# Block-sparse attention and a rational FFN on one core: other PSUM banks for the first scores, paired reads of block numbers, unit factors in one operation

## The chip, the cores and the metric

One core of a Trainium2 chip runs the whole program. The metric is the time of one execution in device microseconds. Three runs of the kernel before gave 828.69, 829.16 and 830.58 us, so the median is 829.16 us.

## The reference

```python
B, H, S, D = 4, 8, 768, 64            # query, key, value; blocks of 32 rows, 24 blocks
scores = q @ k.T / sqrt(D)
mask = near (|i-j| <= 1) | first and last block row and column | 3 sampled blocks per query block
attn = softmax(where(mask, scores, -1e9)) @ v
x = attn.transpose(0, 2, 1, 3).reshape(3072, 512)
h = x @ w_in                          # 512 -> 2048
P = a0 + a1*h + a2*h*h + a3*h*h*h
Q = 1 + |b0|*|h| + |b1|*h*h
out = (P / (Q + 1e-6)) @ w_out        # 2048 -> 512
```

The weights arrive as 64-bit floats and are decoded on the chip.

## The kernel before, in words

The work has three kinds. **Attention** takes two query blocks at a time, a "part" (x = 0, 1, 2, ...; 14 parts per batch, of which three share the two edge blocks that see all keys). For each part PE writes scores into two PSUM banks (`scores`, L817), DVE adds the bias and takes maxima (`maxima`, L829), ACT takes exponentials (L848), PE turns the probabilities (`turn`, L894) and multiplies them with the values (`values`, L940), DVE normalises (L966), PE turns the result (L978), and ACT and DVE write it as two f16 halves, `xh` (L150) and `xl` (L989). In batch 0 the keys of the sampled blocks are copied by POOL from SBUF (`copies`, L761); in later batches SP gathers them. The values are always gathered by SP (L919). Block numbers for both are read from the tile `ix` into registers by a TENSOR_LOAD (`sampled_rows`, L711), one per part and engine, six numbers each.

The **FFN** works on chunks of 256 tokens (c = 0 to 11) in 16 units each (`unit`): the first product in three f16 passes into a bank `ph` (`into`, L1036 to L1038, two halves e = 0, 1), then about ten DVE and ACT operations (L1043 to L1081) that make `gh` (L1071) and `gl` (L1081), then the second product into `acc` (`out_high`, L1093 and L1095; `out_low`, L1099). Four factors per unit (unit scale times 1, |b0|, a1, a3) stand in the tile `fc`, which `factors` fills with four DVE operations per group of units (L1010). There are seven such groups: four of two units each in batch 0, one of eight elements per row for each later batch.

The **weights** are decoded between 17 and 215 us: rows of w_in and w_out pass through DVE (L441, L444, L447) and through conversions that may go to ACT, DVE or POOL (`times`, L150, L152, L154; POOL also L461 and L519).

PSUM has eight banks: two for `acc`, two for `ph`, three named `m` that scores and every transpose share, and one for `av`. Keys of batch 0 are transposed in `ph` banks at the very start; after that the `ph` banks stand unused until the first `into`.

The order on each engine is set ahead of time by a list scheduler in the kernel (`issue`): each `Op` has an engine or several, a price in ns, predecessors, a priority, and slots in rings (`r_sp` for the three `m` banks, `r_ph` for the two `ph` banks). Engines then run their lists strictly in that order. Until the second product begins, the scheduler also puts idle products of an identity on PE (`fill`, L162).

Of the kernel before, what the change touches and what calls it, by code (L numbers as in the profile page):

```python
# [11 lines left out]
F32 = mybir.dt.float32  # L12
# [5 lines left out]
ALU = mybir.AluOpType  # L18
# [6 lines left out]
def kernel(  # L25
# [27 lines left out]
    nc = tc.nc  # L53
    B, H, S, D = q.shape
    DM, DFF = out.shape[1], w_out.shape[0]
    P = 128
    BLK = 32
    NB = S // BLK
    NR = sampled_blocks.shape[1]
# [16 lines left out]
    const = ctx.enter_context(tc.tile_pool(name="const", bufs=1))  # L76
# [8 lines left out]
    ps_h = ctx.enter_context(tc.tile_pool(name="ps_h", bufs=2, space=PSUM))  # L85
# [11 lines left out]
    VE, SC, PO, TE, SY = "DVE", "Activation", "Pool", "PE", "SP"  # L97
# [176 lines left out]
    r_ph, r_sp, r_acc = Ring([None] * 2), Ring(range(3)), Ring([None])  # L274
    r_pr, r_st, r_pT, r_av = Ring([None] * 3), Ring([None] * 4), Ring([None] * PT), Ring(range(2))
# [9 lines left out]
    ix = const.tile([1, NB, NR], I32, name="ix")  # L285


    par = const.tile([P, 8], F32, name="par")
    absb = const.tile([P, 2], F32, name="absb")
    bias = const.tile([P, NB, NS], F32, name="bias")  # L290

    def load_small():
# [4 lines left out]
    def setup():  # L297
        nc.vector.tensor_scalar(out=ix, in0=samp[0:1].rearrange("p i (n w) -> p i n w", w=2)[:, :, :, 0],
                                scalar1=0, scalar2=NB - 1, op0=ALU.max, op1=ALU.min)
        nc.scalar.activation(out=absb, in_=par[:, 4:6], func=AF.Abs)  # L300

        sf = work[:, 2 * NR * NB:3 * NR * NB].rearrange("p (n i) -> p n i", n=NR)
        nc.vector.tensor_copy(out=sf, in_=samp.rearrange("p i (n w) -> p n i w", w=2)[:, :, :, 0])
        ii = work[:, 5 * NR * NB:5 * NR * NB + NB]
        nc.gpsimd.iota(ii, pattern=[[1, NB]], base=0, channel_multiplier=0, allow_small_or_imprecise_dtypes=True)
        dup = work[:, 3 * NR * NB:4 * NR * NB].rearrange("p (n i) -> p n i", n=NR)
        tmp = work[:, 4 * NR * NB:5 * NR * NB].rearrange("p (n i) -> p n i", n=NR)
        for r in range(NR):
            nc.vector.tensor_tensor(out=dup[:, r], in0=sf[:, r], in1=ii, op=ALU.subtract)
        nc.vector.tensor_tensor(out=dup, in0=dup, in1=dup, op=ALU.mult)  # L310
        nc.vector.tensor_scalar(out=dup, in0=dup, scalar1=1.0, scalar2=None, op0=ALU.is_le)
        for edge in (0.0, NB - 1.0):
            nc.vector.tensor_scalar(out=tmp, in0=sf, scalar1=edge, scalar2=None, op0=ALU.is_equal)
            nc.vector.tensor_tensor(out=dup, in0=dup, in1=tmp, op=ALU.max)
        for r in range(1, NR):
            for e in range(r):
                nc.vector.tensor_tensor(out=tmp[:, r], in0=sf[:, r], in1=sf[:, e], op=ALU.is_equal)
                nc.vector.tensor_tensor(out=dup[:, r], in0=dup[:, r], in1=tmp[:, r], op=ALU.max)
        nc.vector.memset(bias, 0.0)
        nc.vector.memset(bias[:, 1, NR:NR + 1], NEG)  # L320
        nc.vector.memset(bias[:, NB - 2, 1:2], NEG)
        for r in range(NR):
            for e in range(2):
                nc.vector.tensor_scalar(out=bias[:, 1 - e:NB:2, r + 5 * e], in0=dup[:, r, 1 - e:NB:2], scalar1=NEG, scalar2=None, op0=ALU.mult)

    s_work = Slot(r_rr)
    o_small = Op(SY, [(475, 1), (475, 1), (475, 1)], load_small, prio=-99, takes=[s_work])
    o_setup = Op(VE, 5300, setup, [o_small], prio=-70, uses=[s_work])


# [43 lines left out]
    banks = [ps_m.tile([P, 512], F32, name=f"m{i}") for i in range(3)]  # L374
# [13 lines left out]
    wscale = const.tile([P, NU], F32, name="wscale")  # L388
# [148 lines left out]
    def block(j):  # L537
        return j + 1 if j < J else 0 if j == J else NB - 1 if j == J + 1 else j - 1
# [12 lines left out]
    kts, xscales, ks_of, v_inv, v_scale, k_done, s_scr, k_evac = {}, {}, {}, {}, {}, {}, {}, {}  # L551
# [10 lines left out]
    def new_pr():  # L562
        return p3.tile([P, 2, 2, NS * BLK], F32, name="pr")
# [135 lines left out]
    parts = []  # L699
    for b in range(B):  # L700
        for j in range(0, NB, 2):
            n = NB // NS if j == J else 1
            parts += [(b, j, s, n) for s in range(n)]
    NX = len(parts)
    rows_of, has = {}, {}

    def sampled_rows(x, eng=mybir.EngineType.SP):

        if (x, eng) not in rows_of:
            i = block(parts[x][1])  # L710
            rows_of[x, eng] = nc.values_load_multi_w_load_instructions(  # L711
                ix[0:1, i:i + 2].rearrange("p i n -> p (i n)"), engines=[eng], min_val=0, max_val=NB - 1,
                skip_runtime_bounds_check_because="clamped when ix was written")[1]
        return rows_of[x, eng]

    def fresh(kind, x, slot):
# [15 lines left out]
    def attention(b, j, prio):  # L732

        i = block(j)
        xs = [x for x, p in enumerate(parts) if p[:2] == (b, j)]
        n = len(xs)
# [3 lines left out]
        prio = [prio + 0.05 * m for m in range(n)]  # L740
        omax, oexp = [], [[], []]
        prs = {}
        for m, x in enumerate(xs):
            def one(m, x):
                p = prio[m]
                s_sp, s_pr = [Slot(r_sp), Slot(r_sp)], Slot(r_pr)
                near = x < KX
                deps = [Q["oq"]]
                kslots = []
                h = {}  # L750
# [42 lines left out]
                    kslots = [s_kg]  # L793

                def scores():
                    h["sp"] = [banks[z.buf].rearrange("p (e s r) -> p e s r", e=2, r=BLK) for z in s_sp]
                    for e in range(2):
                        if near and n > 1:
                            pieces = [(slice(0, NS), kall[:, m * NS:(m + 1) * NS])]
                        elif n > 1:  # L800
                            pieces = [(slice(0, NS), kgs[s_kg.buf][:, 0:NS])]
                        elif near:
                            own = [kxs[:, s_kx.buf, e], kall[:, 0:NB:NB - 1], kall[:, i - 1 + e:i + 2 + e]]
                            pieces, at = [], 0
                            for kx in own if e == 0 else own[1:] + own[:1]:
                                pieces.append((slice(at, at + kx.shape[1]), kx))
                                at += kx.shape[1]
                        elif e == 0:
                            pieces = [(slice(0, NS), kgs[s_kg.buf][:, 0:NS])]
                        else:  # L810
                            pieces = [(slice(0, 2), kgs[s_kg.buf][:, NR:NR + 2]), (slice(2, NS), kgs[s_kg.buf][:, NR + 3:])]
                        q0 = (j + e) % TB * BLK
                        for sl, kx in pieces:
                            for h4 in range(HG):
                                for g in range(2):
                                    rows = slice(g * D, (g + 1) * D)
                                    nc.tensor.matmul(h["sp"][g][h4 * BLK:(h4 + 1) * BLK, e, sl], Q["q"][rows, h4, q0:q0 + BLK], kx[rows, :, h4],  # L817
                                                     start=True, stop=True)
                    if m == 0:
                        d["st"] = p4.tile([P, 40], F32, name="st")  # L820
                    prs[x] = new_pr()

                def maxima(e):
                    def run():
                        st = d["st"]
                        add = bias[:, i + e] if n == 1 else bias[:, 0, 0:1].broadcast_to([P, NS])
                        for g in range(2):
# [5 lines left out]
                    return run  # L833

                o = chain["sc"] = sc_of[x] = Op(TE, 1050 if near else 880, scores, deps, p, behind=chain.get("sc"), takes=s_sp + [s_pr] + ([s_st] if m == 0 else []),
                                     uses=kslots + [Q["slot"]] + ([] if m == 0 else [s_st]))
                o.work = 0.4 if near else 1.0
# [14 lines left out]
                return s_pr, exps  # L852

            d[m] = one(m, x)

        def larger(m):
# [6 lines left out]
        for m, x in enumerate(xs):  # L863
            s_pr, exps = d[m]
# [90 lines left out]
        p = prio[-1] + 3 * 0.1  # L955
# [46 lines left out]
    fcs, o_fc, accs, s_acc, kept = {}, {}, {}, {}, {}  # L1002

    def factors(b, u, n, after, prio):

        def run():
            if b not in fcs:
                fcs[b] = p2.tile([P, 4, NU], F32, name="fc")
            for j, coef in enumerate((1.0, absb[:, 0:1], par[:, 1:2], par[:, 3:4])):
                nc.vector.tensor_scalar(out=fcs[b][:, j, u:u + n], in0=wscale[:, u:u + n], scalar1=v_inv[b], scalar2=coef, op0=ALU.mult, op1=ALU.mult)  # L1010
        for x in range(u, u + n):
            o_fc[b, x] = None
        o = Op(VE, 700, run, after + [o_fc.get((b, 0))], prio)
        for x in range(u, u + n):
            o_fc[b, x] = o

# [169 lines left out]
    for b in range(B):  # L1186
        if b:
            prep(b, when(b))
        for t in range(NT):
            x0 = min(x for x, p in enumerate(parts) if p[0] == b and p[1] // TB == t)  # L1190
            before = prep_q(b, t, -78.95 if b == t == 0 else part_prio(x0) - (3.23 if x0 >= need[0] else 12.17), before)
            for j in range(t * TB, (t + 1) * TB, 2):
                x = next(x for x, p in enumerate(parts) if p[:2] == (b, j))
                attention(b, j, part_prio(x))

    for c, u in order:
        b = c // NCH
# [48 lines left out]
```

## Time and profile before

| | us |
|---|---|
| median of three runs | 829.16 |
| the profiled execution | 828.6 |
| its span, first to last instruction | 826.8 |
| PE busy | 770.6 (93%) |
| DVE busy | 674.9 (82%) |
| ACT busy | 569.7 (69%) |
| POOL busy | 107.5 (13%) |

The profile shows one execution. An engine's busy share is an average over stages with different limits: a share for a stretch is read from the windows below. Where a wait has several causes, the view of waits names the one that came last.

### The profile page before, as it was taken

Reading aid. Unit: us, or ns where it says so; the run is one execution under the profiler, and the core shown is the slowest. Engines: PE = TensorE matmul, PEld = TensorE weight load, DVE = VectorE, ACT = ScalarE, POOL = GpSimd, SP = SyncE. Lnnn points to the kernel's source line nnn. Section 1 sums busy time; section 2 is a strip of 40 time slices with the busy share of each in tenths; the row PEclk is TensorE's granted clock in tenths of the full one; section 3 lists DMA queues with packets and bytes.
Section 4 is the critical chain, followed back from the end, with each engine's and each line's share of the span. In section 5 each row is a group of like instructions: output and inputs, shape, how many; then the busy total and the mean of one; then the engine's idle time right before and its main releaser. Section 6 shows DMA issues by size and latency. Waiting matters only on the chain.

```text
span 826.8 us, 27468 instructions
## 1 busy us (share of the span) xinstructions
PE 770.6 (93%) x10859; PEld 557.3 (67%) x10943; DVE 674.9 (82%) x1580; ACT 569.7 (69%) x1264; POOL 107.5 (13%) x149
## 2 busy tenths in 40 slices
PE   8798918898999999999999999999999999999997
PEld 4556605676677768677777767677777767767774
DVE  2788999899988885788878884887888886887886
ACT  2676777677866769677576759676676758766563
POOL 3547485613100000000000000000000000000000
PEclk9999969899999999999999999999999999999999
DMA  7988874537566957545636757635555436220000
GB/s 210 242 220 238 233 231 138 163 87 189 142 154 165 214 162 194 162 123 162 160 108 164 191 145 196 173 96 157 144 151 149 117 111 182 76 65 2 1 26 26
DMA packets 224416, 121.29 MB, mean 147 GB/s; under 512 B 62624, under 2 KB 214048, under 8 KB 224288
## 3 DMA queue, kind: packets, MB, share of 16 engines
q1 hardware_dynamic: 223136, 115.34, 51.6%
q0 software_dynamic: 1152, 4.19, 1.6%
q8 instruction: 86, 1.41, 0.8%
q14 instruction: 42, 0.34, 0.1%
HBM read 108.47 MB, written 11.01 MB: 145 GB/s over the span
## 4 chain that ended last, share of the span: by engine, by line
PE 81%; DVE 7%; DMA 4%; issue 3%; ACT 2%; POOL 2%; SPq 1%; ACTq 0%; POOLq 0%; DVEq 0%
PE acc L1093 11%; PE ph L1036 9%; PE acc L1095 9%; PE acc L1099 9%; PE ph L1037 9%; PE ph L1038 9%; PE m L817 7%; PE av L940 6%; PE m L894 6%; PE acc L162 3%; DMA vg<-in_v_dram 2%; PE m L556 2%; DMA wl<-in_moe_w_out_dram 1%; PE m L978 1%; POOL wo_h L154 1%
## 5 line engine op out<-in xcount | busy, mean ns | idle before, releaser
L1037 PE MATMUL ph<-xl,wi 128*128 128x256 f16 x768 | 210.5, 274 | 3.1 <-DVE xl L989 3.1
L1036 PE MATMUL ph<-xh,wi 128*128 128x256 f16 x768 | 210.9, 275 | 1.4 <-DVE tt L1053 1.4
L1038 PE MATMUL ph<-xh,wi 128*128 128x256 f16 x768 | 210.7, 274 | 0.0
L1043 ACT ACTIVATE sq<-ph,fc 128x512 f32<-128x512 f32 x96 | 65.9, 687 | 112.6 <-PE ph L1038 112.4
L1093 PE MATMUL acc<-wo_h,gh 128*128 128x512 f32 x384 | 114.5, 420 | 18.7 <-DVE gh L1071 18.0
L848 ACT ACTIVATE pr<-pr,st 128x256 f32<-128x256 f32 x224 | 110.7, 501 | 14.3 <-DVE st L860 14.3
L1060 DVE SCALAR_TENSOR_TENSOR ab<-sq,absb,ab 128x512 f32<-128x512 f32 x96 | 73.2, 763 | 37.1 <-ACT ab L1057 36.9
L829 DVE CUSTOM_DVE_ANT_1 pr<-m,bias 128x256 f32<-128x256 f32 x224 | 83.2, 418 | 22.3 <-PE m L817 22.1
L1099 PE MATMUL acc<-wo_b,gl 128*128 128x512 bf16 x368 | 95.4, 379 | 3.4 <-issue 2.1
L1095 PE MATMUL acc<-wo_l,gh 128*128 128x512 bf16 x316 | 86.5, 384 | 4.6
L1036 PEld LDWEIGHTS <-wi 128*128 128x128 f16 x768 | 75.9, 99 | 21.4 <-issue 5.1
L1071 DVE SCALAR_TENSOR_TENSOR gh<-tt,par,rr 128x512 fp32r<-128x512 f32 x96 | 72.3, 753 | 19.8 <-ACT rr L1067 11.2
L1093 PEld LDWEIGHTS acc<-wo_h,gh 128*128 128x128 f32 x384 | 66.0, 191 | 32.7 <-issue 19.6
L150 ACT ACTIVATE pT<-m 128x512 f32<-128x512 f32 x112 | 64.1, 596 | 34.0 <-PE m L894 32.7
L1037 PEld LDWEIGHTS <-wi 128*128 128x128 f16 x768 | 75.6, 98 | 12.7 <-issue 0.2
L1038 PEld LDWEIGHTS <-wi 128*128 128x128 f16 x768 | 75.5, 98 | 12.6 <-issue 3.4
L1047 ACT ACTIVATE tt<-ph,par,fc 128x512 f32<-128x512 f32 x96 | 74.8, 779 | 0.3 <-DVE gl L1081 0.2
L1050 DVE TENSOR_TENSOR tt<-tt,sq 128x512 f32<-128x512 f32 x96 | 66.9, 697 | 9.4 <-ACT tt L1047 9.4
L1057 ACT ACTIVATE ab<-ph,fc 128x512 f32<-128x512 f32 x96 | 65.6, 683 | 11.2 <-DVE tt L1077 10.5
L1077 DVE SCALAR_TENSOR_TENSOR tt<-tt,par,ab 128x512 f32<-128x512 f32 x96 | 72.2, 752 | 0.5
L894 PE MATMUL m<-ident,pr 128*128 128x128 f32 x448 | 69.6, 288 | 2.9 <-ACT kt L150 2.3
L1053 DVE SCALAR_TENSOR_TENSOR tt<-ph,fc,tt 128x512 f32<-128x512 f32 x96 | 71.4, 744 | 0.8
(130 smaller groups left out, 1221.7 us busy)
## 6 DMA issues: line engine op xcount, KB each, us to landing
vg<-in_v_dram SPq DMA_DIRECT2D x312, 64.0 KB, 2.9
vg<-in_v_dram SPq DMA_DIRECT2D x88, 192.0 KB, 3.6
kall<-ks SPq DMA_DIRECT2D x138, 64.0 KB, 1.9
wl<-in_moe_w_out_dram SPq DMA_DIRECT2D x16, 512.0 KB, 4.8
vg<-in_v_dram SPq DMA_DIRECT2D x12, 512.0 KB, 5.1
kall<-ks SPq DMA_DIRECT2D x23, 256.0 KB, 3.7
ldq<-in_q_dram SPq DMA_DIRECT2D x20, 256.0 KB, 3.4
out_dram<-ld SPq DMA_DIRECT2D x20, 256.0 KB, 2.4
```

The source lines that it names most:

```text
L829: nc.vector.tensor_tensor_reduce(out=prs[x][:, e, g].rearrange("p (s r) -> p s r", r=BLK), in0=h["sp"][g][:, e], in1=add.rearrange("p (s o ...
L848: nc.scalar.activation(out=prs[x][:, e, g], in_=prs[x][:, e, g], func=AF.Exp, scale=SCALE, bias=st[:, 12 + y:13 + y], accum_out=st[:, 16 + ...
L894: nc.tensor.transpose(pp[:, jj * P:(jj + 1) * P], pr[:, e, g, kt:NS * BLK:2], ident)
L1036: nc.tensor.matmul(o, wh, xh[:, :, cc], start=(cc == 0), stop=False)
L1037: nc.tensor.matmul(o, wh, xl[:, :, cc], start=False, stop=False)
L1038: nc.tensor.matmul(o, wl, xh[:, :, cc], start=False, stop=(cc == NCC - 1))
L1047: nc.scalar.activation(out=d["tt"], in_=d["ph"], func=AF.Identity, scale=d["cst"][:, 3:4], bias=par[:, 2:3])
L1060: nc.vector.scalar_tensor_tensor(out=d["ab"], in0=d["sq"], scalar=absb[:, 1:2], in1=d["ab"], op0=ALU.mult, op1=ALU.add)
L1071: nc.vector.scalar_tensor_tensor(out=d["gh"], in0=d["tt"], scalar=par[:, 0:1], in1=d["rr"], op0=ALU.add, op1=ALU.mult)
L1093: nc.tensor.matmul(acc, g, wo_h[:, f], start=(new and e == 0), stop=False)
L1095: nc.tensor.matmul(acc, g, wo_l[:, f], start=False, stop=False)
L1099: nc.tensor.matmul(acc, g, wo_b[:, f], start=False, stop=(last and e == 1))
```

## The change

Three edits:

1. The scores of parts 0 to 4 go to the two `ph` banks instead of to two of the three `m` banks, so that in those parts transposes have the three `m` banks to themselves.
2. One TENSOR_LOAD reads twelve block numbers for two successive parts where the parts' blocks follow each other; the second part then issues none. SP has 24 such loads where it had 44, POOL 6 where it had 11.
3. `factors` is one operation over a `[128, 4, n]` tile in place of four, from a new tile `coefs` that `setup` fills with four small DVE operations; its price in the scheduler is 180 ns where it was 700.

```diff
@@ -287,6 +287,7 @@
 
     par = const.tile([P, 8], F32, name="par")
     absb = const.tile([P, 2], F32, name="absb")
+    coefs = const.tile([P, 4], F32, name="coefs")
     bias = const.tile([P, NB, NS], F32, name="bias")
 
     def load_small():
@@ -298,6 +299,10 @@
         nc.vector.tensor_scalar(out=ix, in0=samp[0:1].rearrange("p i (n w) -> p i n w", w=2)[:, :, :, 0],
                                 scalar1=0, scalar2=NB - 1, op0=ALU.max, op1=ALU.min)
         nc.scalar.activation(out=absb, in_=par[:, 4:6], func=AF.Abs)
+        nc.vector.memset(coefs[:, 0:1], 1.0)
+        nc.vector.tensor_copy(out=coefs[:, 1:2], in_=absb[:, 0:1])
+        nc.vector.tensor_copy(out=coefs[:, 2:3], in_=par[:, 1:2])
+        nc.vector.tensor_copy(out=coefs[:, 3:4], in_=par[:, 3:4])
 
         sf = work[:, 2 * NR * NB:3 * NR * NB].rearrange("p (n i) -> p n i", n=NR)
         nc.vector.tensor_copy(out=sf, in_=samp.rearrange("p i (n w) -> p n i w", w=2)[:, :, :, 0])
@@ -708,9 +713,13 @@
 
         if (x, eng) not in rows_of:
             i = block(parts[x][1])
-            rows_of[x, eng] = nc.values_load_multi_w_load_instructions(
-                ix[0:1, i:i + 2].rearrange("p i n -> p (i n)"), engines=[eng], min_val=0, max_val=NB - 1,
+            two = x + 1 < NX and parts[x + 1][0] == parts[x][0] and parts[x + 1][3] == 1 and block(parts[x + 1][1]) == i + 2
+            got = nc.values_load_multi_w_load_instructions(
+                ix[0:1, i:i + (4 if two else 2)].rearrange("p i n -> p (i n)"), engines=[eng], min_val=0, max_val=NB - 1,
                 skip_runtime_bounds_check_because="clamped when ix was written")[1]
+            rows_of[x, eng] = got[:2 * NR]
+            if two:
+                rows_of[x + 1, eng] = got[2 * NR:]
         return rows_of[x, eng]
 
     def fresh(kind, x, slot):
@@ -743,7 +752,8 @@
         for m, x in enumerate(xs):
             def one(m, x):
                 p = prio[m]
-                s_sp, s_pr = [Slot(r_sp), Slot(r_sp)], Slot(r_pr)
+                early_x = x < 5
+                s_sp, s_pr = [Slot(r_ph if early_x else r_sp) for _ in range(2)], Slot(r_pr)
                 near = x < KX
                 deps = [Q["oq"]]
                 kslots = []
@@ -793,7 +803,7 @@
                     kslots = [s_kg]
 
                 def scores():
-                    h["sp"] = [banks[z.buf].rearrange("p (e s r) -> p e s r", e=2, r=BLK) for z in s_sp]
+                    h["sp"] = [(ps_h.tile([P, 512], F32, name="ph") if early_x else banks[z.buf]).rearrange("p (e s r) -> p e s r", e=2, r=BLK) for z in s_sp]
                     for e in range(2):
                         if near and n > 1:
                             pieces = [(slice(0, NS), kall[:, m * NS:(m + 1) * NS])]
@@ -1006,11 +1016,11 @@
         def run():
             if b not in fcs:
                 fcs[b] = p2.tile([P, 4, NU], F32, name="fc")
-            for j, coef in enumerate((1.0, absb[:, 0:1], par[:, 1:2], par[:, 3:4])):
-                nc.vector.tensor_scalar(out=fcs[b][:, j, u:u + n], in0=wscale[:, u:u + n], scalar1=v_inv[b], scalar2=coef, op0=ALU.mult, op1=ALU.mult)
+            nc.vector.scalar_tensor_tensor(out=fcs[b][:, :, u:u + n], in0=coefs.rearrange("p (j o) -> p j o", o=1).broadcast_to([P, 4, n]), scalar=v_inv[b],
+                                           in1=wscale[:, u:u + n].rearrange("p (o u) -> p o u", o=1).broadcast_to([P, 4, n]), op0=ALU.mult, op1=ALU.mult)
         for x in range(u, u + n):
             o_fc[b, x] = None
-        o = Op(VE, 700, run, after + [o_fc.get((b, 0))], prio)
+        o = Op(VE, 180, run, after + [o_fc.get((b, 0))], prio)
         for x in range(u, u + n):
             o_fc[b, x] = o
 
```

Because prices and rings change, the scheduler sets another order on every engine from about the first score on. Counted over the whole program: PE has 134 idle products where it had 135 (127 where it had 128 ahead of the first `into`). Seven weight conversions more are on POOL (10 `wi<-wo`, 14 `dw<-wi` and 10 `wo_h<-dw` where there were 7, 12 and 8); DVE has five fewer (two `dw<-wi`, one `dw<-wl`, one `wi<-wo_l`, one cast to `wo_h`), ACT two fewer. After the 1146th of DVE's 1553 instructions the orders are alike.

The first place is DVE's, where the first factors of batch 0 stand just behind the scale of the values (`sc`) and ahead of the first `xl`. Before:

```order
L356 TENSOR_SCALAR sc_1035<-sc_1035 128x1
L660 COPY xscale<-sc_1035 128x1
L1010 TENSOR_SCALAR fc<-wscale,sc_1035 128x2
L1010 TENSOR_SCALAR fc<-wscale,sc_1035,absb 128x2
L1010 TENSOR_SCALAR fc<-wscale,sc_1035,par 128x2 x2
L498 TENSOR_REDUCE sums<-sums 128x1
L966 TENSOR_TENSOR xn<-av,st 128x256
L989 SCALAR_TENSOR_TENSOR xl_117<-m_102,xscale,xh_116 128x512
```

And with the change:

```order
L361 TENSOR_SCALAR sc_1057<-sc_1057 128x1
L665 COPY xscale<-sc_1057 128x1
L1019 SCALAR_TENSOR_TENSOR fc<-coefs,sc_1057,wscale 128x4x2
L503 TENSOR_REDUCE sums<-sums 128x1
L976 TENSOR_TENSOR xn<-av,st 128x256
L999 SCALAR_TENSOR_TENSOR xl_118<-m_102,xscale,xh_117 128x512
```

Nothing moved here; four operations became one, with two tensors from SBUF as inputs where each of the four had one.

The second place is also DVE's: the fourth `xl`, which completes the input of chunk 1 and so lets PE begin that chunk's first product. Before, it is instruction 310 of DVE's list, 52 behind the fourth `gh`:

```order
L355 TENSOR_SCALAR scw<-scw 128x1
L356 TENSOR_SCALAR scw<-scw 128x1
L872 TENSOR_SCALAR st<-st 128x4
L502 COPY wscale<-scw 128x1 x2
L875 RECIPROCAL st<-st 128x4
L1010 TENSOR_SCALAR fc<-wscale,sc_1035 128x2
L1010 TENSOR_SCALAR fc<-wscale,sc_1035,absb 128x2
L1010 TENSOR_SCALAR fc<-wscale,sc_1035,par 128x2 x2
L989 SCALAR_TENSOR_TENSOR xl_119<-m_103,xscale,xh_118 128x512
```

With the change it is instruction 279, 21 behind the fourth `gh`:

```order
L976 TENSOR_TENSOR xn<-av,st 128x256
L452 SCALAR_TENSOR_TENSOR wi<-wo_b,wi 128x512
L449 SCALAR_TENSOR_TENSOR wi<-wo_l,wi 128x512
L446 TENSOR_SCALAR wi<-wi 128x512
L452 SCALAR_TENSOR_TENSOR wi<-wo_l,wi 128x512
L449 SCALAR_TENSOR_TENSOR wi<-wo_b,wi 128x512
L999 SCALAR_TENSOR_TENSOR xl_120<-m_103,xscale,xh_119 128x512
```

The maxima of the next part, two groups of factors, the sums of a softmax and seven decoding steps stood ahead of it and now stand behind it.

The third place is PE's, the second product of unit 2 of chunk 0 (the third pass through L1093). Before, it follows straight on the last product of unit 1:

```order
L1099 LDWEIGHTS gl
L1099 MATMUL acc<-wo_b,gl 128x512
L1093 MATMUL acc<-wo_h,gh 128x512 x4
L1095 LDWEIGHTS gh
L1095 MATMUL acc<-wo_l,gh 128x512
```

With the change:

```order
L1109 LDWEIGHTS gl
L1109 MATMUL acc<-wo_b,gl 128x512
L904 MATMUL m_102<-ident,pr 128x128 x8
L950 MATMUL av<-vg_113,pT 32x64 x32
L904 MATMUL m_102<-ident,pr 128x128 x4
L561 MATMUL m_102<-ident,ld 128x128 x4
L950 MATMUL av<-vg_111,pT 32x64 x32
L1103 MATMUL acc<-wo_h,gh 128x512 x4
```

Turns and value products of the edge part, which came after that product, now come ahead of it.

## Rows read from the trace of the kernel before

**Rows 1.** Busy us of PE, PEld, DVE, ACT, POOL by stretch; clock, DMA share, GB/s.

```profile
60.00:80.00 20.00, 16.95 (x348) 12.62 (x347) 17.22 (x45) 12.86 (x33) 17.24 (x27) 0.97 0.77 225
80.00:160.00 80.00, 53.46 (x920) 38.87 (x923) 72.95 (x162) 57.96 (x137) 50.26 (x46) 0.84 0.67 195
160.00:235.00 75.00, 70.71 (x1022) 51.49 (x1019) 74.44 (x164) 55.91 (x120) 15.91 (x15) 1.00 0.56 145
235.00:310.00 75.00, 74.34 (x1076) 54.49 (x1083) 64.02 (x162) 50.81 (x113) 0.00 (x0) 1.00 0.70 174
310.00:750.00 440.00, 432.96 (x6075) 319.53 (x6130) 347.14 (x822) 316.68 (x711) 0.00 (x0) 1.00 0.52 142
```

**Rows 2.** Waits of PE from 60 to 235 us: total, times, longest.

```profile
PE acc L1093 <- DVE gh L1071: 18.0, 2, 17.6
PE ph L1037 <- DVE xl L989: 3.1, 1, 3.1
...
PE m L894 <- ACT kt L150: 2.3, 1, 2.3
```

**Rows 3.** The chain that ended last, 101 to 122 us: start, us, what.

```profile
101.42 7.89 POOL wo_h L154
...
113.87 0.65 POOL dw L154
...
114.55 0.87 DVE dw L441
...
121.28 0.67 DVE gh L1071
```

**Rows 4.** Busy time of line L1010 (factors) alone, by stretch.

```profile
50.00:62.00 12.00, 4.70 (x8) 1.00 0.78 198
130.00:150.00 20.00, 3.61 (x8) 0.84 0.52 144
220.00:225.00 5.00, 0.80 (x4) 1.00 0.45 137
398.00:401.00 3.00, 0.80 (x4) 1.00 0.66 181
584.00:588.00 4.00, 0.81 (x4) 1.00 0.59 168
```

**Rows 5.** Line L1010 over the span: shortest, median and longest in ns.

```profile
L1010 DVE TENSOR_SCALAR fc<-wscale,sc x7: 216/226/958, 53.0 to 585.4; 128x2 f32<-128x2 f32 x4, 128x8 f32<-128x8 f32 x3
L1010 DVE TENSOR_SCALAR fc<-wscale,sc,absb x7: 274/280/1201, 53.6 to 585.6; 128x2 f32<-128x2 f32 x4, 128x8 f32<-128x8 f32 x3
```

**Rows 6.** DVE in order of time, one decoding step twice.

```profile
107.20 0.68 DVE L447 SCALAR_TENSOR_TENSOR wi<-wo_b,wi 128x512 int32<-128x512 int32 x1
...
109.76 1.75 DVE L444 SCALAR_TENSOR_TENSOR wi<-wo_b,wi 128x512 int32<-128x512 int32 x1
```

**Rows 7.** DVE's conversions by line: busy us, mean ns, idle before.

```profile
L154 DVE TENSOR_SCALAR dw<-wi,scw 128x512 f32<-128x512 f32 x4 | 4.9, 1239 | 3.4 <-POOL wi L519 2.0 <-POOL wo_l L461 1.4
L154 DVE TENSOR_SCALAR dw<-wl 128x512 f32<-128x512 f32 x2 | 1.9, 956 | 0.0
L154 DVE TENSOR_SCALAR wi<-wo_l 128x512 f32<-128x512 f32 x2 | 1.2, 584 | 0.0
L152 DVE CAST wo_h<-dw 128x512 fp32r<-128x512 f32 x2 | 0.8, 404 | 0.0
```

**Rows 8.** POOL's conversions to wo_h over the span: shortest, median and longest in ns.

```profile
L154 POOL TENSOR_SCALAR wo_h<-dw x8: 618/1048/7886, 82.2 to 208.4; 128x512 fp32r<-128x512 f32 x8
```

**Rows 9.** PE's idle products ahead of the first product, in order of time.

```profile
59.52 2.76 PE L162 MATMUL acc<-ident 128*128 128x512 f16 x12
...
65.86 0.27 PE L1036 MATMUL ph<-xh,wi 128*128 128x256 f16 x1
```

**Rows 10.** The loads of block numbers: shortest, median, longest.

```profile
L711 SPq TENSOR_LOAD <-ix x44: 1262/1273/1710, 11.1 to 689.2; - x44
L711 POOLq TENSOR_LOAD <-ix x11: 1384/1391/1634, 14.2 to 155.1; - x11
```

**Rows 11.** PE's only wait for gathered values, of the whole span.

```profile
PE av L940 <- DMA vg<-in_v_dram: 0.2, 1, 0.2
```

**Rows 12.** DVE behind the setup, in order of time.

```profile
11.65 0.69 DVE L152 COPY kall<-ph 128x512 f32<-128x512 f32 x1 [2.50 <-PE ph L556]
...
20.59 0.42 DVE L829 CUSTOM_DVE_ANT_1 pr<-m,bias 128x256 f32<-128x256 f32 x1 [5.77 <-PE m L817]
```

## The prediction, as it was put on record before any run of the change

> **What bounds the kernel now.** I read the busy time by stretch first. From 235 us on, PE is busy for all but a few us: 74.3 of 75, then 433.0 of 440 [rows 1]. That part is a fixed amount of PE work, and only what happens before it can move its start. Before it, PE is idle for 33.9 us between 60 and 235 us (3.0, 26.5 and 4.3 in the three stretches), while DVE is busy for 147.4 of the 155 us from 80 to 235 us [rows 1]. So the early part is DVE's, and the reader should see there an engine that does three jobs at once: decoding weights, maxima of attention, and the FFN's element-wise work.
>
> Then the waits: over half of PE's idle time is one wait of 17.6 us for `gh`, the first factor of the second product; behind it come 3.1 us for `xl` and 2.3 us for a turned key [rows 2]. Last, the chain through the long wait: a POOL conversion that took 7.89 us where its like take 1.05 [rows 3, 8], then a conversion on POOL, a decoding step on DVE that needs it, and the `gh` that stands behind that in DVE's list [rows 3]. So PE's wait is DVE's lateness, and some of DVE's lateness is POOL's.
>
> **The change, part by part.**
>
> Factors. Twenty-eight DVE operations go and seven come. The five groups ahead of 235 us are busy for 4.70 (two groups), 3.61 (two groups) and 0.80 us, 9.1 in all; the other two, at 0.80 and 0.81 us, lie where DVE has over 90 of 440 us free and PE sets the pace, so they cost nothing now and give nothing back [rows 1, 4]. Undisturbed, a group takes 0.80 us, as the third row has it [rows 4]. The first four groups took 8.31 us, 2.1 each, while POOL was at work beside them; the shortest single operation was 0.22 us, the longest 1.20 [rows 5].
>
> The trace has no operation like the new one, so I bound it: from below by the shortest factor operation, 0.22 us [rows 5]; from above by a DVE step that normally takes 0.68 us and took 1.75 beside POOL [rows 6]. Five of them cost 1.1 to 8.75 us. I take 0.6 us each, 3.0 in all, near the lower end: it has 8 to 32 elements per row, and in the first four groups more than half of the time is disturbance, which one operation meets once where four met it up to four times. Gain 9.1 - 3.0 = **6.1 us**, with 8.0 and 0.4 as ends.
>
> The row of 1.20 us shows that a factor operation with one tensor input already waits for POOL [rows 5]. [...]
>
> The four small operations in the setup cost DVE some 0.5 us, and they wait for |b|, under 1 us more. DVE waits 2.50 us for PE before the second key tile, and 5.77 us before the first maxima [rows 12]; the cover is larger than the cost, so I take 0. Without that cover it would be 1.5 us.
>
> Weight conversions that change engine. DVE loses five: two at 1.24 us, and 0.96, 0.58 and 0.40 [rows 7], 4.4 us. POOL gains seven. Each may hold up one DVE step, by nothing or by as much as the 1.07 us by which one step was stretched from 0.68 to 1.75 [rows 6], 0 to 7.5 us. I take the middle, 3.7, because rows of both kinds stand side by side. Net gain **0.7 us**, with 4.4 and -3.1 as ends.
>
> Banks. Ahead of the first product at 65.86 us the scheduler fills PE's free time with idle products, such as 12 of them in 2.76 us just before the sixth part's scores [rows 9]. If transposes had been in the scores' way, fewer of them would be left with the change; but the new order has 127 of them ahead of that product where there were 128. So the PE time up to the first product hardly changes: 0, with a gain of 1 as the end. The risk is that the first product needs a `ph` bank that the scores of part 4 still hold; those scores were done 6 us before it [rows 9], so I count nothing.
>
> Block numbers. Forty-four loads of 1.27 us on SP become 24, and 11 of 1.39 us on POOL become 6 [rows 10]. No row shows a load of twelve numbers. Between the same time and twice it, SP's sum goes from 56 us to between 31 and 61, and POOL's from 15 to between 8 and 17. Who would feel it? PE waited for gathered values once, 0.2 us [rows 11], and POOL has 30 of 80 us free between 80 and 160 us [rows 1]. I take 0, with a loss of 1.4 as the end (the first pair's copies land later by one load).
>
> The order. The turns and value products placed ahead of the third second product run inside PE's 17.6 us wait instead of behind it, and the fourth `xl` comes 31 instructions earlier relative to the fourth `gh`. DVE's total of work does not change by that, so in a stretch that DVE bounds I count 0. The end on the good side is PE's waits there, 3.1 + 2.3 = 5.4 us [rows 2].
>
> **The sum.** 6.1 + 0.7 = 6.8 us. The profiled execution took 828.6 us (span 826.8), 0.6 us below the median of 829.16. 828.6 - 6.8 = 821.8; on the median's scale **822.4 us**. The ends of the terms that don't exclude each other give 816 to 828 for this case.
>
> **The rivals.**
>
> 1. The wait for `xl` goes too. For it: the order puts `xl` well ahead of the decoding steps that delayed it, and PE has the turns that it needs done earlier. Against it: DVE must still do those steps before the units that use them. Price: 5.4 us more, 822.4 - 5.4 = 817.0; if the 7.89 us conversion also takes the usual 1.05, 6.8 less, 810. This case covers 810 to 817, with 816 as its likeliest.
>
> 2. Nothing to measure. Every new factor operation is held by POOL as the longest step was (1.75 us), which leaves 0.4 us of 6.1, while the loads and banks lie beside other work as above. 829.16 - 0.4 - 0.7 = 828.1. For it: rows 5 and 6 show such holds just where the factors stand. Against it: only some of the old rows were held.
>
> 3. Slower, by POOL. A conversion on POOL that stands beside an unbroken run of DVE steps takes 7.89 us [rows 3], 6.8 more than its like [rows 8], with the decoding and PE's second product behind it. POOL now has seven conversions more, two of them this very kind. One further hold on the chain cancels the gain (829.2); the second makes 829.2 + 6.8 = 836. It decides from the point where more than one further hold lies on the chain that PE waits for. Against it: one of eight such conversions was held so long, and in the new list DVE has less work between the units.
>
> **How the numbers follow.** A measurement of this kernel can tell 0.2%, 1.7 us, from no change. The forecast has 0.50, rival 1 has 0.20, rival 2 and a single hold together 0.12, rival 3 has 0.18. Faster: 0.50 + 0.20 = 0.70; same 0.12; slower 0.18. The range 813 to 832 takes in the forecast's own 816 to 828, the better part of rival 1, rival 2 and the mild side of rival 3; below it lies some 0.05, above it some 0.12. Cases of both signs share it, so the forecast's own range, 816 to 828, is the narrower statement.
>
> **What would show it.** Right: seven factor operations of 0.3 to 1.7 us in place of 28; PE's wait for `gh` at the third second product shorter by about 4 us; DVE's busy stretch ending near 228 us instead of 235; the stretches after it unchanged; 24 and 6 loads, with no wait of PE for values above 1 us. Wrong: a POOL conversion of several us on the chain a second time, PE waits of several us at a place that had none, or a first product that waits for maxima in a `ph` bank. If the whole gain lay ahead of 65 us, the banks would have done what I count at nothing.

## The result, and the profile after

The changed kernel took 835.88 us (median of 13 runs, 833.19 to 841.59) beside 829.28 us for the kernel before (13 runs, 827.78 to 834.38). The ratio is 1.0073, with a 95% interval of [1.0057, 1.0089]: by it, about 6.1 us slower. The forecast was 822.4 us, and 832 was the upper end of its range.

The stretches of [rows 1], now (PE, PEld, DVE, ACT and POOL busy, clock, DMA share, GB/s):

```profile
60.00:80.00 20.00, 17.86 (x385) 12.92 (x387) 14.74 (x47) 14.31 (x34) 16.10 (x24) 1.00 0.82 201
80.00:160.00 80.00, 55.98 (x914) 40.47 (x903) 76.47 (x165) 54.33 (x130) 44.56 (x47) 0.87 0.77 214
160.00:235.00 75.00, 69.05 (x1092) 50.24 (x1091) 74.92 (x155) 58.09 (x128) 32.87 (x29) 1.00 0.61 136
235.00:310.00 75.00, 74.62 (x1104) 54.11 (x1102) 63.06 (x152) 52.45 (x116) 0.00 (x0) 1.00 0.81 178
310.00:750.00 440.00, 435.72 (x6125) 317.62 (x6124) 344.57 (x815) 313.17 (x700) 0.00 (x0) 1.00 0.58 143
```

PE and DVE look much as before. What changed in every row are the last two columns: from 310 to 750 us the transfers moved 143 GB/s where they had moved 142, but kept the DMA engines busy for 0.58 of the time, not 0.52. The same bytes cost 11% more transfer time.

The rows that answer to [rows 5], [rows 8] and [rows 10] (shortest, median, longest in ns):

```profile
L1019 DVE SCALAR_TENSOR_TENSOR fc<-coefs,sc,wscale x7: 207/245/670, 61.0 to 593.4; 128x8 f32<-128x8 f32 x4, 128x32 f32<-128x32 f32 x3
```

```profile
L154 POOL TENSOR_SCALAR wo_h<-dw x10: 617/1040/1665, 88.1 to 201.8; 128x512 fp32r<-128x512 f32 x10
```

```profile
L717 SPq TENSOR_LOAD <-ix x24: 1281/2472/2680, 12.0 to 690.0; - x24
L717 POOLq TENSOR_LOAD <-ix x6: 1385/2723/2937, 15.7 to 138.2; - x6
```

The factors came out shorter than the 0.6 us each that were taken (0.21 to 0.67 us, 0.25 by the median), no conversion to `wo_h` on POOL took 7.89 us, and a load of twelve numbers takes twice a load of six: 2.47 against 1.27 us on SP.

PE's longest waits from 60 to 235 us, for [rows 2]:

```profile
PE acc L1103 <- DVE gh L1081: 10.5, 1, 10.5
...
PE m L904 <- ACT ab L1067: 4.0, 1, 4.0
PE m L904 <- ACT pr L858: 2.7, 1, 2.7
```

The wait for `gh` shrank by 7 us as other PE work moved into it. But the time had gone before it. The first second product, where PE first multiplies by decoded w_out rows (PE, in order of time), before:

```profile
89.79 0.47 PE L1093 MATMUL acc<-wo_h,gh 128*128 128x512 f32 x1 [0.48 <-DVE gh L1071]
```

and with the change:

```profile
95.40 0.94 PE L1103 MATMUL acc<-wo_h,gh 128*128 128x512 f32 x3
```

So 5.6 us were missing at 90 us. DVE behind the setup, for [rows 12], is late already:

```profile
13.07 0.69 DVE L152 COPY kall<-ph 128x512 f32<-128x512 f32 x1 [2.56 <-PE ph L561]
...
22.89 0.42 DVE L839 CUSTOM_DVE_ANT_1 pr<-ph,bias 128x256 f32<-128x256 f32 x1 [5.77 <-PE ph L827]
```

The first maxima start at 22.89 us where they started at 20.59. DVE still waits for PE ahead of both, so DVE's own four new operations are not what it is late by. The kernel shift32 below, which lacks them, starts its first maxima at 22.89 us too.

### The profile page after: what moved, and what is told of

It is laid out like the page before. It is cut to its first block, busy times and chain, and to the rows that moved or that the text cites. A ratio compares the mean times of both kernels' runs of the same rounds, so it can differ in the third digit from the quotient of the medians.

```text
span 834.9 us, 27503 instructions
## 1 busy us (share of the span) xinstructions
PE 781.8 (94%) x10942; PEld 559.9 (67%) x10942; DVE 672.2 (81%) x1558; ACT 567.6 (68%) x1262; POOL 112.5 (13%) x156
## 3 DMA queue, kind: packets, MB, share of 16 engines
q1 hardware_dynamic: 223136, 115.34, 57.4%
## 4 chain that ended last, share of the span: by engine, by line
PE 78%; DVE 12%; issue 3%; DMA 3%; ACT 2%; SPq 1%; ACTq 0%; DVEq 0%
PE acc L1103 10%; PE ph L1046 9%; PE acc L1109 9%; PE acc L1105 9%; PE ph L1048 9%; PE ph L1047 9%; PE m L827 6%; PE m L904 5%; PE av L950 5%; PE acc L162 2%; PE m L561 2%; DMA ldq<-in_q_dram 1%; PE m L988 1%; DVE gh L1081 1%; DMA vg<-in_v_dram 1%
## 5 line engine op out<-in xcount | busy, mean ns | idle before, releaser
L1109 PE MATMUL acc<-wo_b,gl 128*128 128x512 bf16 x384 | 99.6, 382 | 2.7 <-DVE gl L1091 2.7
L1105 PE MATMUL acc<-wo_l,gh 128*128 128x512 bf16 x384 | 100.5, 385 | 0.0
L1081 DVE SCALAR_TENSOR_TENSOR gh<-tt,par,rr 128x512 fp32r<-128x512 f32 x96 | 75.0, 781 | 19.6 <-ACT rr L1077 10.9
L839 DVE CUSTOM_DVE_ANT_1 pr<-m,bias 128x256 f32<-128x256 f32 x204 | 76.0, 418 | 12.6 <-PE m L827 12.2
L904 PEld LDWEIGHTS m<-ident,pr 128*128 128x128 f32 x448 | 64.3, 207 | 17.2 <-ACT ab L1067 4.2
```

The costliest lines, as they stand in the source:

```text
L839: nc.vector.tensor_tensor_reduce(out=prs[x][:, e, g].rearrange("p (s r) -> p s r", r=BLK), in0=h["sp"][g][:, e], in1=add.rearrange("p (s o ...
L904: nc.tensor.transpose(pp[:, jj * P:(jj + 1) * P], pr[:, e, g, kt:NS * BLK:2], ident)
L1081: nc.vector.scalar_tensor_tensor(out=d["gh"], in0=d["tt"], scalar=par[:, 0:1], in1=d["rr"], op0=ALU.add, op1=ALU.mult)
L1105: nc.tensor.matmul(acc, g, wo_l[:, f], start=False, stop=False)
L1109: nc.tensor.matmul(acc, g, wo_b[:, f], start=False, stop=(last and e == 1))
```

## The experiments

Each edit of the change can be made alone. The first four kernels do that, under two theories of the cause: A, the paired loads; B, the banks. Each ratio is to the kernel before, run beside it, with its 95% interval. A profile is one execution, up to some 3 us off its kernel's median, so times read from profiles are a sign and the ratios are the measure.

**pairs_only**: the kernel before with only this.

```diff
-            rows_of[x, eng] = nc.values_load_multi_w_load_instructions(ix[0:1, i:i + 2] ...
+            got = nc.values_load_multi_w_load_instructions(ix[0:1, i:i + (4 if two else 2)] ...
...
```

> The kernel before with the paired loads alone; the order on every engine is that of before. Theory A (the loads: a load of twelve numbers takes 2.5 to 2.7 us, so the first part of a pair gets its gathers and copies 1.2 us later, and the second part's gathers then come in a bunch that delays other transfers): 4 to 6 us over the kernel before, and the first second product near 95 us, not 90. Theory B (the banks: scores in two ph banks make a slower early order): within 1 us of the kernel before, first second product near 90 us.

Measured: 1.0008 [0.9996, 1.0019], first second product at 92.26 us. Theory A falls as the whole cause.

**no_pairs**: the changed kernel with that hunk taken back.

> The changed kernel without the paired loads: banks and factors in one operation, the order that of the changed kernel. Theory A: the first second product back near 90 us, and the gain of the factors and of the shorter wait for gh shows, 3 to 7 us below the kernel before (822 to 826). Theory B: 4 to 7 us over the kernel before, first second product near 95 us.

Measured: 1.0045 [1.0027, 1.0063], first second product at 95.73 us: 3.7 us over, just short of theory B's range and against theory A.

**banks_only**: the kernel before with only the other ring and banks.

```diff
-                s_sp, s_pr = [Slot(r_sp), Slot(r_sp)], Slot(r_pr)
+                s_sp, s_pr = [Slot(r_ph if early_x else r_sp) for _ in range(2)], Slot(r_pr)
...
```

> The kernel before with the first scores in the ph banks alone (the scheduler sets another order for it). Theory A: within 2 us of the kernel before, first second product near 90 us. Theory B: 4 to 7 us over the kernel before, first second product at 94 us or later.

Measured: 1.0017 [1.0002, 1.0032], so at most 2.7 us where theory B asked for 4 to 7: it falls too as the whole cause. But its other sign came true: the first second product is at 95.52 us, as late as with the change. With another order a late first second product need not cost the program that time.

**factors_same_order**: the kernel before with `coefs` and the single operation, priced as before.

```diff
-            for j, coef in enumerate((1.0, absb[:, 0:1], par[:, 1:2], par[:, 3:4])):
...
+            nc.vector.scalar_tensor_tensor(out=fcs[b][:, :, u:u + n], in0=coefs...
```

> The kernel before with the factors in one operation, at the old price of 700 ns, so that the order is that of before. Both theories: the first second product earlier by the 3 to 4 us that the first two groups of factors save on DVE, if DVE bounds the way there, and the whole 3 to 6 us below the kernel before; within 1 us of it if DVE's time there is covered or the wait for gh gives it back.

Measured: 1.0030 [1.0014, 1.0046], first second product at 95.31 us. This is the surprise among the four: the kernel does less on DVE in the same order, and is slower. The DMA part of the profiles sorts the kernels. The queue that carries the data kept the engines busy for 57.4, 58.1 and 57.8% of the span in the three kernels that have the tile `coefs` (the change, no_pairs, factors_same_order), and for 51.6, 50.9 and 51.0% in the three that do not (before, pairs_only, banks_only). The queue's bytes and packets are the same.

That points at where tiles stand. In the compiled programs the 8 bytes per partition of `absb` and the 16 of `coefs` take 32 each, so `coefs` moves every tile allocated behind it by 32. Starts modulo 512, read from the programs (no view of the profile shows them):

```
tile                                     before   change
kall, wi                                    480        0
vg (values), ldq (queries), tt, ab, sq        0       32
ld (raw keys, values, outputs)              256      288
wl (raw w_out)                              384      416
```

Theory C: the address. The rival, D: the four operations, or the new form.

**shift32**: the kernel before and a tile that nothing reads or writes. No instruction differs.

```diff
     absb = const.tile([P, 2], F32, name="absb")
+    const.tile([P, 8], F32, name="pad")
```

> The kernel before with one unused 32-byte tile where the change put coefs: no instruction differs, but every later SBUF tile starts 32 bytes further on (value tiles at a multiple of 64 plus 32, where they stood at a multiple of 64). Theory C (the address: transfers into tiles that start off a multiple of 64 take longer): the queue's share of the 16 DMA engines 57 to 58% instead of 51 to 52, values 3.8 us to landing instead of 2.9, and 3 to 8 us over the kernel before. Theory D (the loss is the setup's four small operations or the factors' new form, not an address): share 51 to 52%, within 1 us of the kernel before.

Measured: 1.0077 [1.0050, 1.0104], first second product at 94.73 us. An unused tile costs as much as the whole change. The data queue (packets, MB, share), and the median us to landing of values and of the first raw keys (last column), before:

```profile
q1 hardware_dynamic: 223136, 115.34, 51.6%
...
vg<-in_v_dram SPq DMA_DIRECT2D x312, 64.0 KB, 2.9
...
tt<-in_k_dram SPq DMA_DIRECT2D x2, 256.0 KB, 4.1
ab<-in_k_dram SPq DMA_DIRECT2D x2, 256.0 KB, 4.3
sq<-in_k_dram SPq DMA_DIRECT2D x2, 256.0 KB, 4.1
```

with the change:

```profile
q1 hardware_dynamic: 223136, 115.34, 57.4%
...
vg<-in_v_dram SPq DMA_DIRECT2D x312, 64.0 KB, 3.8
...
tt<-in_k_dram SPq DMA_DIRECT2D x2, 256.0 KB, 4.7
ab<-in_k_dram SPq DMA_DIRECT2D x2, 256.0 KB, 5.3
sq<-in_k_dram SPq DMA_DIRECT2D x2, 256.0 KB, 5.1
```

and in shift32:

```profile
q1 hardware_dynamic: 223136, 115.34, 58.0%
...
vg<-in_v_dram SPq DMA_DIRECT2D x312, 64.0 KB, 3.8
...
tt<-in_k_dram SPq DMA_DIRECT2D x2, 256.0 KB, 4.6
ab<-in_k_dram SPq DMA_DIRECT2D x2, 256.0 KB, 5.3
sq<-in_k_dram SPq DMA_DIRECT2D x2, 256.0 KB, 5.2
```

Values land 0.9 us later, the first keys 0.5 to 1.1 us later, in both alike.

**shift64**: `[P, 16]` in place of `[P, 8]`.

> The same with an unused tile of 64 bytes: value tiles at a multiple of 64 again, but no longer at one of 256 or 512. Theory C with a grain of 64 bytes: share 51 to 52%, within 1 us of the kernel before. Theory C with a grain of 256 bytes or more: share 57% or more and 3 us or more over the kernel before, as with 32. Theory D: within 1 us.

Measured: 1.0065 [1.0041, 1.0089]; values are at a multiple of 64 again and yet slow:

```profile
q1 hardware_dynamic: 223136, 115.34, 56.5%
...
vg<-in_v_dram SPq DMA_DIRECT2D x312, 64.0 KB, 3.6
```

**shift256**: `[P, 64]`.

> The kernel before with one unused tile of 256 bytes: value tiles and query rows start at a multiple of 256 that is not one of 512. Theory C with a grain of 256 bytes: share of the queue 51 to 53%, values 2.9 to 3.1 us to landing, within 2 us of the kernel before (the key tile and the w_out rows move to other odd starts). Theory C with a grain of 512 bytes (the size of one row of a transfer): share 56% or more, values 3.6 to 3.8 us, 4 us or more over the kernel before.

Measured: 0.9996 [0.9977, 1.0014]:

```profile
q1 hardware_dynamic: 223136, 115.34, 50.8%
...
vg<-in_v_dram SPq DMA_DIRECT2D x312, 64.0 KB, 2.9
...
sq<-in_k_dram SPq DMA_DIRECT2D x2, 256.0 KB, 3.7
```

For these tiles, starts of 0 and 256 past a multiple of 512 were fast (values land after 2.9 us in both), 32 and 64 slow (3.8 and 3.6 us). A packet here has 517 bytes on average (115.34 MB in 223,136) and took 30.6 ns before, 34.6 in shift32, 33.6 in shift64 and 30.1 in shift256 (share x 16 engines x span / packets, with spans 826.8, 832.2, 829.9 and 827.6 us). Why a start at 32 or 64 costs time and one at 256 does not, no run shows.

It was not so for every transfer. The gathers of later keys into `kall` write rows of 512 bytes too, and the start of `kall` went from 480 to 0 with the change. Yet their 64 KB gathers land after 1.9 us before, 2.0 with the change and 1.9 in shift32. What sets the values apart no run shows.

**after_same_addr** and **factors_same_addr**: `coefs` goes into the unused rest of `absb`'s 32 bytes, so that nothing moves.

```diff
-    absb = const.tile([P, 2], F32, name="absb")
-    coefs = const.tile([P, 4], F32, name="coefs")
+    small = const.tile([P, 8], F32, name="small")
+    absb, coefs = small[:, 0:2], small[:, 4:8]
```

> The changed kernel with coefs in the unused rest of absb's 32 bytes, so that every other tile stands where it stood in the kernel before; instructions and order are those of the changed kernel. Theory C: share back at 51 to 52%, the first second product at 90 to 92 us, and the forecast gain shows at least in part: 2 to 7 us below the kernel before. Theory D: still 5 to 7 us over it.

Measured: 1.0012 [0.9996, 1.0029], share 51.0%. The loss is gone, the forecast gain (theory C's 2 to 7 us here) has not come.

> The factors in one operation alone, in the order of before, with coefs in absb's 32 bytes. Theory C: share 51 to 52%, 1 to 6 us below the kernel before, as far as DVE's 6 us saved are not given back at the next wait. Theory D: 2 to 3 us over the kernel before, as factors_same_order was.

Measured: 0.9974 [0.9957, 0.9991], 2.2 us faster than before.

**no_pairs_same_addr**: the changed kernel at the old addresses, without the paired loads.

> The changed kernel with the old addresses and without the paired loads. If the paired loads cost what the changed kernel at the old addresses lacks of the factors' gain: 1 to 3 us below the kernel before, near 827. If the banks and the new order cost it: 829 to 832, as the changed kernel at the old addresses.

Measured: 0.9973 [0.9956, 0.9990], as the factors alone: banks and new order together neither give nor take beyond the error. Against after_same_addr, the paired loads cost 0.39%, 3.2 us, in this order; the two intervals do not meet.

**pool_pairs_same_addr** and **sp_pairs_same_addr** pair the loads on one engine only.

```diff
-            two = x + 1 < NX and ...
+            two = x + 1 < NX and eng == mybir.EngineType.Pool and ...
```

> The changed kernel at the old addresses with paired loads on POOL alone (SP has its 44 single loads). If POOL's paired loads, ahead of the copies of keys that the first scores wait for, cost the 3 us by which the paired loads are dearer there: 829 to 831, first second product near 91 us. If SP's cost it: near 827, first second product near 87.5 us.

> The same with paired loads on SP alone (POOL has its 11 single loads). If SP's paired loads, ahead of the gathers and of the weight rows queued behind them, cost the 3 us: 829 to 831, first second product near 91 us. If POOL's cost it: near 827, first second product near 87.5 us.

Measured: 0.9982 [0.9967, 0.9998] with POOL's pairs, first second product at 87.93 us; 0.9998 [0.9982, 1.0013] with SP's, at 91.20 us (87.34 with neither, 91.11 with both). SP's carry most of it, as far as the intervals, which overlap, and these times go. SP in order of time; L929 are the gathers that need the first load, L687 the load of the second queries behind them. With single loads on SP:

```profile
10.27 0.43 SPq L925 DMA_DIRECT2D vg<-in_v_dram  x1
12.47 1.35 SPq L929 DMA_DIRECT2D vg<-in_v_dram  x3
13.93 0.40 SPq L687 DMA_DIRECT2D ldq<-in_q_dram  x1
```

With pairs on SP:

```profile
10.63 0.43 SPq L925 DMA_DIRECT2D vg<-in_v_dram  x1
14.04 1.53 SPq L929 DMA_DIRECT2D vg<-in_v_dram  x3
15.69 0.46 SPq L687 DMA_DIRECT2D ldq<-in_q_dram  x1
```

The longer load stands ahead of the gathers and of everything behind them on SP's queue: the queries are issued 1.8 us later. PE does not wait for these, however: it turns them only at 28.50 and 33.53 us, and from 14 to 60 us its waits name no transfer. Where the profiles part is a pause of PE in the second part's scores, for which they name no cause ("issue"). Its end, with POOL's pairs and with SP's:

```profile
25.51 0.63 PE L827 MATMUL ph<-kall,qt 64*32 64x96 f32 x35 [2.02 <-issue]
...
28.25 0.90 PE L827 MATMUL ph<-kall,qt 64*32 64x96 f32 x34 [4.53 <-issue]
```

By then the kernel with SP's pairs is 2.7 us behind, of 3.3 at the first second product; with neither pair the pause is 2.69 us and ends at 25.66. The path from SP's queue to this pause is not shown; more on it at the end.

**values_shift32** and **rest_shift32** split the shift: the value tiles alone, or everything behind them.

```diff
+    const.tile([P, 8], F32, name="pa")
     vgs = [const.tile([P, H, 2 * D], F32, name=f"vg{i}") for i in range(4)]
+    const.tile([P, 120], F32, name="pb")
```

> The kernel before with only the four value tiles moved 32 bytes off; every other tile that transfers write keeps its start modulo 512. If the gathers of values carry the loss: 4 us or more over the kernel before, share 55% or more, values 3.6 us or more to landing, query rows at 3.4. If the query rows and the raw rows of weights and keys carry it: within 1.5 us.

> The complement: the value tiles stay, every tile behind them (query rows, raw rows of keys, values and weights, later keys) starts 32 bytes off. If the gathers of values carry the loss: within 1.5 us of the kernel before, share 52 to 54%. If the others carry it: 4 us or more over it.

Measured: 1.0032 [1.0018, 1.0046] and 1.0038 [1.0024, 1.0052], so both expectations were half right; the sum is near that of shift32. values_shift32:

```profile
q1 hardware_dynamic: 223136, 115.34, 58.2%
...
vg<-in_v_dram SPq DMA_DIRECT2D x312, 64.0 KB, 3.8
...
sq<-in_k_dram SPq DMA_DIRECT2D x2, 256.0 KB, 4.1
```

rest_shift32:

```profile
q1 hardware_dynamic: 223136, 115.34, 51.8%
...
vg<-in_v_dram SPq DMA_DIRECT2D x312, 64.0 KB, 2.9
...
sq<-in_k_dram SPq DMA_DIRECT2D x2, 256.0 KB, 5.2
```

The values make nearly all of the added transfer time, but only half of the loss. They are 312 transfers of 64 KB, 88 of 192 and 12 of 512, 86,016 rows of 512 bytes. If all of the 882 us that the queue's engine time grew by (58.2% and 51.6% of 16 spans) fell on them, each took about 10 ns more, an estimate. The few transfers of keys and queries at the start hardly show in the share, yet the work behind them comes later: with only those and what stands behind the values moved, the first maxima start at 22.88 us, as in shift32; with only the values at 21.30, and at 21.06 in shift256. The first second products, at 93.97 and 91.80 us, are less telling: the first of these profiles is of the slowest of that kernel's ten runs, 833.69 us, the second of the fastest, 829.61.

**all_aligned** and **factors_all_aligned**: also the key tile, `wl`, the later keys' tiles and `ld` at multiples of 512.

```diff
+    wscale = const.tile([P, DFF // P // 2], F32, name="wscale")
     bias = const.tile([P, NB, NS], F32, name="bias")
...
-    wscale = const.tile([P, NU], F32, name="wscale")
...
```

> The kernel before, instructions and order unchanged, with wscale allocated ahead of bias and four paddings, so that also the key tile (which stood at 480 past a multiple of 512), the FFN's weight rows wl (384 past) and the later keys' xkg and ld (320 past) start at multiples of 512. Theory C: share below 50%, wl and xkg land sooner than 4.8 and 1.9 us, first second product 1 us or more earlier, 1 to 4 us below the kernel before. If only the values' and queries' address counted: within 1 us.

> The same with the factors in one operation at the old price (order of before). Theory C and the factors' own gain add: 3 to 6 us below the kernel before (823 to 826). If the two meet the same wait they do not add: about 2 us below, as the factors alone.

Measured: 1.0004 [0.9986, 1.0022], a miss, and 0.9968 [0.9949, 0.9986]. The share fell to 50.4%, but `wl` lands after 4.9 us, where it took 4.8, and `xkg` after 1.8, where it took 1.9: these transfers did not get faster to speak of. The four kernels that beat the kernel before (factors_same_addr at 826.99 us, no_pairs_same_addr at 827.44, factors_all_aligned at 827.09, pool_pairs_same_addr at 827.64) cannot be told apart.

## Why the prediction was wrong

The loss of 0.73% splits into three parts: addresses, 1.0073 - 1.0012 = 0.61% (5.1 us); paired loads, 1.0012 - 0.9973 = 0.39% (3.2 us); the rest, -0.27% (-2.2 us). 5.1 + 3.2 - 2.2 = 6.1 us. The forecast was -6.8 us; the 12.9 us between are 5.1, 3.2 and the 4.6 us by which the gain fell short. The parts depend on what else is changed: the addresses cost 0.56% with the factors alone (1.0030 - 0.9974), 0.72% without paired loads (1.0045 - 0.9973) and 0.77% alone (shift32); the paired loads 0.08% in the old order (pairs_only) and 0.28% in the new one with the tiles moved (1.0073 - 1.0045).

**Setup, taken as 0: the step that failed.** I priced four small operations and not the tile that they fill. The operations themselves (0.50 us by their durations, behind a wait of 1.05 us for |b|) are covered, as I argued from [rows 12]: with them and the old addresses, DVE still waits 1.08 us for PE at the second key copy (factors_same_addr), and that kernel is faster than before. The tile moved every destination behind it, and the 5.1 us that this cost lay in no term of the sum.

**Block numbers, taken as 0 with a loss of 1.4 as the end: the second step that failed.** The row I lacked shows the upper of my bounds, twice the time. (With it SP's sum stays near 56 us and POOL's near 15, not 61 and 17: four of the 24 loads and one of the 6 stay single.) I had looked at who waits for gathered values in the whole span [rows 11], where PE waits 0.2 us, and not at what the longer load holds up: all that stands behind it on SP's queue. Which of these transfers PE feels stays open; what the profiles show is the pause in the second part's scores, 4.53 us with SP's pairs and 2.69 with none. The six numbers more took (2.47 - 1.27) / 6 = 0.20 us each on SP, so one load of 2.47 us in place of two of 1.27 saved 0.07 us.

**Factors, 6.1 us: right for DVE, mis-sized for the program.** In factors_same_addr the five groups ahead of 235 us took 2.72 us of DVE where they had taken 9.11 [rows 4]: 6.4 us saved. The new form was held beside POOL, but not for the 1.75 us of my upper bound: an operation that began inside one of POOL's waited for the rest of it. With the change the factors from 60.99 to 61.66 us stand beside a POOL operation from 60.48 to 61.64, those from 156.90 to 157.42 beside one from 156.23 to 157.39; they took 0.67 and 0.52 us, and undisturbed, one takes 0.21 us. The old form was held as well (53.56 to 54.76 us, beside POOL work that ends at 54.74), as the prediction read from [rows 5], and one operation met one hold where four met several. But for the program, alone and at the old addresses, they give 2.2 us. The premise that failed is "the early part is DVE's". The two groups from 50 to 62 us took 1.31 us where they had taken 4.70 [rows 4], yet the first second product came only 0.6 us earlier (89.23), and that of unit 2, where the long wait for `gh` is, at 121.35 us, not 122.09. Nor did DVE's busy stretch end earlier with the change: 74.92 of 75 us from 160 to 235. The chain that ended last, before:

```profile
81.00 5.80 DMA vg<-in_v_dram
86.87 6.17 DMA wl<-in_moe_w_out_dram
```

and with the factors' edit:

```profile
87.57 4.75 DMA wl<-in_moe_w_out_dram
...
100.68 7.89 POOL wo_h L154
...
120.54 0.68 DVE gh L1076
121.35 2.05 PE acc L1098 x4
```

Ahead of that product's decoding on DVE stands a transfer of w_out rows, issued at 86.87 and 87.57 us. DVE's saved time did not bring it forward. That the rest of the 6.1 us ends there is read from these chains; no run moved the transfer alone. My rows had it in view: a DMA share of 0.77 from 60 to 80 us [rows 1], which I did not use.

**Banks, 0, and the order, 0: right.** No_pairs_same_addr equals the factors alone. The conversions that changed engine, 0.7 us, are within that error and were not tried alone.

**The rivals.** Rival 3 gave 836 us, and 835.9 was measured, by luck and for another reason: the longest conversion to `wo_h` on POOL took 1.67 us. Its row deserves less than I gave it. In shift32 the 7.89 us conversion does not occur (the longest took 1.13 us), and PE's wait for `gh` is still 16.7 us. A number that fits does not show a mechanism. Rival 1's wait of the first product for `xl`, 3.1 us, is gone from PE's waits, but a turn (L561) waits 1.8 us for `xl`, and waits for `ab` and `pr` of 4.0 and 2.7 us came in, at places that had none, which the prediction gave as a sign of being wrong.

## What to carry to other kernels

A new tile can move every tile allocated behind it: compare the addresses of the two compiled programs, and put small additions into the unused rest of an existing tile, or at the end. To see whether a loss is the address's, add an unused tile of the same size to the old kernel; in the profile the sign here was a larger DMA share at about the same GB/s. Judge it by the time of whole runs: half of the loss came from transfers that hardly show in the share. Before merging two loads, ask what stands behind the first one on its queue, and whether the merged load is shorter than the sum (here 2.47 us in place of two of 1.27).

## What the runs showed of the hardware that was not expected

With the value tiles 32 or 64 bytes past a multiple of 512, the data queue's packets took 13 and 10% more time on average (34.6 and 33.6 ns, not 30.6); with them 256 past it was 30.1 ns. The 64 KB gathers into `kall`, in rows of 512 bytes, took no longer to land from 480 past (1.9 us before) than from 0 (2.0 with the change). A TENSOR_LOAD of six numbers took 1.27 us on SP, one of twelve 2.47. The five factor operations of the new form that began inside a POOL operation (in the change and in factors_same_addr) ended 0.01 to 0.03 us behind it and took 0.52 to 0.96 us; undisturbed ones took 0.21 to 0.25.

And the profile gives a pause of PE in the middle of the second part's scores to nothing that it waits for ("issue"): 2.62 us before, 4.27 in shift32, 3.72 in both halves of that shift. Slower transfers are not needed for it: it is 4.17 us in after_same_addr and 4.53 in sp_pairs_same_addr, at the old addresses. In each of the eighteen traces one packet of the queue that the DMA view calls "instruction" (q8) begins 2.5 to 3.0 us ahead of the pause's end: at 23.25 us for 25.98 before, 26.45 for 29.28 with the change, 27.15 for 29.92 in shift32, 25.68 for 28.25 in sp_pairs_same_addr. In the nine with a pause of 3.6 us or more it begins at 25.2 us or later, though in two with a shorter one (pairs_only, factors_all_aligned) it does so too. No run moved that packet alone, so whether the pause waits for it is not shown.
